# 108 tiny zero products among TensorE's first filler in an RWKV attention and spatial-gating kernel

## The chip, the cores and the metric

The kernel runs on one core of one Trainium2 chip. The time is device microseconds from one launch to the end. Besides the timed runs there is one profiled execution; the trace, from which all rows below are taken, is of that execution.

## The reference

Two stages follow each other. The first is a linear recurrence with a decay per channel, over 4 batches, 8 heads, 768 steps and 48 channels a head:

```
cur   = (u * k_t) outer v_t
y_t   = r_t . (state + cur)
state = w_t * state + k_t outer v_t
```

The second takes y as x (768 rows of 384 values per batch) and is a gated two-layer network with mixing along the sequence:

```
h = relu(x @ w_in);  u, v = halves of h
v_n = (v - mean(v)) / sqrt(var(v) + 1e-6)
v_s = w_spatial @ v_n + b_spatial          (along the 768 steps)
out = (u * v_s) @ w_out
```

## The kernel before

The recurrence is cut into chunks of 128 steps, so there are 24 slots (4 batches of 6 chunks). A slot turns the decays into running products with two scans on VectorE (L442, L452), scales k and r by them (L455, L457), transposes k on TensorE (L514, tile pt), forms the state's increments (L572, tile pp), the scores within a half chunk (L497, tile pp), and adds state and score products into the tile pyw (L526). The slots up to the sixth also do a small product for the bonus term (L427, tile pg). For the first eight slots TensorE helps to form the low part of the result (L621). After each slot its rows go through the second half of w_in (tile ph, L631 to L633: each product of full precision is made of three, from high and low parts). When a batch's six chunks are there, the first half of w_in (tile pu), the spatial mixing (tile pv), the gate and w_out (tile po) follow. The weights are split into high and low parts on the chip as they arrive (tiles d_, e_, wi, ws, wo).

Nothing is decided at run time. The long table PLAN gives each of the program's operations an engine and a start time, `plan` sorts them, and `issue` writes them in that order to five instruction streams; SyncE's stream issues all loads and stores, in order, each after the operation that frees its buffer.

One thing is put between: `fill`. It walks through the sorted operations and, where the plan leaves TensorE idle, calls `warm(n)` for n products of zeros: a load of the zero tile zk and a bf16 product of 128 x 320 into pw, a part of the pyw tile that nobody reads. 73 such products stand in the program, all in its first sixth; the first 23 stand at the very start, before the first transposes of slot 0. They are instructions as any other: TensorE does them in order, whether or not it would have been idle.

TensorE's stream is by far the longest: 6019 weight loads and 6019 matmuls in the trace. An fp32 product of the program is two loads and two matmuls there (the 16 products of L572 in a slot are 32 matmuls), a transpose, an fp32r or a bf16 product is one of each.

Of the kernel before, what the change touches and what calls it, by code (L numbers as in the profile page):

```python
# [116 lines left out]
GAP, FILL_TO = 0.2, 5  # L117

WINDOW, DUTY, UNIT = 3.41, 0.95, 0.15

EARLY = 8

# [8 lines left out]
Q = 32  # L131
# [84 lines left out]
def kernel(  # L216
# [14 lines left out]
    nc = tc.nc  # L231
# [39 lines left out]
    pw = pyw[:, :, KX:, :].rearrange("p x a t -> p x (a t)")  # L271
# [597 lines left out]
    count = [0]  # L869

    def warm(n):
        z = zk.bitcast(BF16)
        for _ in range(n):
            nc.tensor.matmul(pw[:, count[0] % 2], z[:, :P], z[:, :pw.shape[-1]], start=count[0] < 2, stop=True,
                             skip_group_check=True)
            count[0] += 1

    def fill(order):
        t, runs = 1.9, []

        def busy(a, b):
            return sum(max(0.0, min(e, b) - max(s, a)) for s, e in runs)

        for o in order:
            if o.on == "T":
                s, took = o.start, o.eng["T"]
                if t < last.start:
                    n = int(min((DUTY * WINDOW - busy(s - WINDOW, s)) / UNIT + 0.99, (s - t - GAP) / UNIT))
                    if n > 0:
                        warm(n)  # L890
                        runs.append((t, t + n * UNIT))
                runs.append((s, s + 0.85 * took))
                t = max(t, s + took)
            yield o

    def range_check():
# [17 lines left out]
        return bad  # L914

    op({"T": 0.1}, lambda: warm(1), w=[("pw", 0)])
    for j in range(2):
        op({"S": 0.45}, lambda j=j: nc.sync.dma_start(
# [6 lines left out]
    for i in range(NS):  # L925
# [22 lines left out]
        if i == FILL_TO:  # L948
            prog.last = last = op({"T": 0.1}, lambda: warm(1), r=[(vn[0, c][0], 0)], w=[("pw", 0)])
# [72 lines left out]
```

## Time and profile before

| | us |
|---|---|
| median of 3 runs (lowest to highest) | 372.14 (371.58 to 374.35) |
| the profiled execution's own time | 373.94 |
| its span, first to last instruction | 372.2 |
| TensorE matmuls busy | 356.9 (96%), x6019 |
| VectorE busy | 246.9 (66%) |
| ScalarE busy | 192.0 (52%) |
| GpSimd busy | 112.6 (30%) |
| DMA, read and written over the span | 126 GB/s |

The profiled execution is 1.80 us slower than the median of the runs, and 1.7 us lie outside its span. Busy times of TensorE overlap from one instruction to the next, so a busy share of 96% does not say that it could not be faster; idle time ahead of an instruction, and what ended it, is read from the timeline.

### The profile page before, as it was taken

How to read it: one execution, taken by the hardware profiler on the slowest of the kernel's cores; microseconds unless marked ns; L12 is line 12 of the kernel's file. 1: busy time of each engine (PE TensorE's matmuls, PEld its weight loads, DVE VectorE, ACT ScalarE, POOL GpSimd, SP SyncE). 2: the span in 40 equal slices, each digit the busy share in tenths (PEclk: the TensorE clock that was granted, in tenths of full speed). 3: DMA queues.
4: the chain of work that ended last, by engine and by line, in shares of the span. 5: the costliest groups of instructions: out<-in, count | busy, mean ns of one | idle time of the engine just before them, and what ended most of it. 6: DMA issues, size and time to landing. Idle time of an engine off the chain costs nothing.

```text
span 372.2 us, 13843 instructions
## 1 busy us (share of the span) xinstructions
PE 356.9 (96%) x6019; PEld 320.0 (86%) x6019; DVE 246.9 (66%) x486; ACT 192.0 (52%) x517; POOL 112.6 (30%) x141
## 2 busy tenths in 40 slices
PE   7699899999999999999999989999999999999995
PEld 4467678899889998998989978999899998999995
DVE  7869969998895875947837767748648571323231
ACT  2648788996347378731644348551445074622122
POOL 2427431023235043273064330380351034021030
PEclk9969999999999999999999999999999999999999
DMA  8857756684543545342534545325423150110211
GB/s 198 258 149 212 221 174 214 195 239 125 163 132 98 179 143 173 111 140 70 160 94 123 169 137 162 95 78 153 140 66 94 44 155 4 37 49 0 91 39 67
DMA packets 33024, 47.91 MB, mean 129 GB/s; under 512 B 3265, under 2 KB 21825, under 8 KB 32961
## 3 DMA queue, kind: packets, MB, share of 16 engines
q1 hardware_dynamic: 32960, 47.00, 43.2%
q8 instruction: 48, 0.79, 0.9%
q14 instruction: 16, 0.12, 0.1%
HBM read 42.27 MB, written 4.72 MB: 126 GB/s over the span
## 4 chain that ended last, share of the span: by engine, by line
PE 81%; DMA 8%; issue 3%; DVE 2%; ACT 2%; SPq 1%; POOL 1%; POOLq 0%; DVEq 0%; ACTq 0%
PE pv L631 9%; PE pyw L526 9%; PE pv L632 8%; PE pv L633 8%; PE po L631 5%; PE po L633 5%; PE po L632 5%; PE ph L631 4%; PE pu L631 4%; PE ph L633 4%; PE ph L632 4%; DMA rr<-in_tr_dram 4%; PE pu L632 4%; PE pu L633 4%; PE pp L497 4%
## 5 line engine op out<-in xcount | busy, mean ns | idle before, releaser
L631 PE MATMUL pv<-ws,vh 128*128 128x384 f32 x192 | 67.0, 349 | 0.4 <-DVE t L737 0.3
L632 PE MATMUL pv<-ws,vh 128*128 128x384 f32 x192 | 64.9, 338 | 0.0
L633 PE MATMUL pv<-ws,vl 128*128 128x384 f32 x192 | 64.8, 338 | 0.0
L737 DVE TENSOR_TENSOR t<-pv,b_sb 128x384 f32<-128x384 f32 x32 | 17.5, 552 | 36.7 <-PE pv L633 34.5
L631 PEld LDWEIGHTS pv<-ws,vh 128*128 128x128 f32 x192 | 36.0, 188 | 2.0 <-DVE t L737 0.5
L632 PEld LDWEIGHTS pv<-ws,vh 128*128 128x128 f32 x192 | 36.1, 188 | 0.2
L633 PEld LDWEIGHTS pv<-ws,vl 128*128 128x128 f32 x192 | 36.0, 188 | 0.0
L631 PE MATMUL pu<-xT,wi 128*128 128x384 f32 x96 | 33.9, 353 | 0.2 <-DVE dg L469 0.2
L631 PE MATMUL po<-wo,gh 128*128 128x384 f32 x96 | 33.1, 345 | 0.0
L632 PE MATMUL pu<-xT,wi 128*128 128x384 f32 x96 | 32.5, 338 | 0.0
L633 PE MATMUL pu<-xT,wi 128*128 128x384 f32 x96 | 32.4, 338 | 0.0
L633 PE MATMUL po<-wo,gl 128*128 128x384 f32 x96 | 32.3, 337 | 0.0
L632 PE MATMUL po<-wo,gh 128*128 128x384 f32 x96 | 32.3, 337 | 0.0
L500 DVE COPY_PREDICATED As<-mask,pp 128x512 f32<-128x512 int32 x24 | 17.7, 739 | 19.2 <-POOL As L483 6.0
L442 DVE TENSOR_TENSOR_SCAN F<-W,zz 112x512 f32<-112x512 f32 x24 | 29.1, 1212 | 1.9 <-ACT zz L454 1.0
L631 PE MATMUL ph<-wi,xT 128*128 128x512 f32 x72 | 30.0, 417 | 0.0
L452 DVE TENSOR_TENSOR_SCAN W<-W,zz 112x512 f32<-112x512 f32 x24 | 29.1, 1213 | 0.4
L741 ACT CAST gh<-t 128x384 fp32r<-128x384 f32 x32 | 16.1, 510 | 25.5 <-POOL t L739 16.1
L633 PE MATMUL ph<-wi,xT 128*128 128x512 f32 x72 | 28.4, 395 | 0.0
L632 PE MATMUL ph<-wi,xT 128*128 128x512 f32 x72 | 28.3, 394 | 0.0
L599 POOL TENSOR_TENSOR SA<-S,prod 112x256 f32<-112x256 f32 x18 | 13.9, 773 | 44.8 <-DVE S L597 39.9
L660 ACT ACTIVATE hv<-ph 128x512 f32<-128x512 f32 x24 | 14.3, 597 | 25.4 <-PE ph L633 25.4
(184 smaller groups left out, 824.6 us busy)
## 6 DMA issues: line engine op xcount, KB each, us to landing
N<-in_nat_dram SPq DMA_DIRECT2D x18, 384.0 KB, 3.5
Nw<-in_gt_dram SPq DMA_DIRECT2D x16, 384.0 KB, 3.6
W<-in_tr_dram SPq DMA_DIRECT2D x24, 224.0 KB, 3.9
kk<-in_tr_dram SPq DMA_DIRECT2D x24, 224.0 KB, 3.2
rr<-in_tr_dram SPq DMA_DIRECT2D x24, 224.0 KB, 3.6
v<-in_nat_dram SPq DMA_DIRECT2D x24, 192.0 KB, 3.5
out_dram<-ot SPq DMA_DIRECT2D x24, 192.0 KB, 3.3
wst<-in_w_spT_dram SPq DMA_DIRECT2D x12, 192.0 KB, 3.8
```

The source lines that it names most:

```text
L442: op({"V": 1.22}, lambda: nc.vector.tensor_tensor_scan(flat(F())[:, ::-1], W[:, 2:][:, ::-1], flat(zz[:R])[:, ::-1], 0.0, ALU.mult, ALU.ma ...
L452: op({"V": 1.22}, lambda: nc.vector.tensor_tensor_scan(W[:, :n], W[:, :n], flat(zz[:R]), 0.0, ALU.mult, ALU.max), r=[("zz", 0)], w=[wk])
L497: nc.tensor.matmul(pa[ts, j, g, :], kk()[rs, g, ts], rr()[rs, g, ts], start=True, stop=True)
L500: op({"V": 0.73}, lambda: nc.vector.copy_predicated(As().rearrange("p (g j) t -> p j g t", j=2), mask.unsqueeze(1).unsqueeze(1).broadcast_ ...
L526: nc.tensor.matmul(py[Q * n:Q * (n + 1), x, k_, :], a, b, start=(x, n) not in seen, stop=True, skip_group_check=True)
L599: op({"V": 0.42, "G": 0.617}, lambda e: e.tensor_tensor(new, S0, Wc.unsqueeze(2).broadcast_to([R, G, E2]), ALU.mult), r=[("S0",), ("Wc", i ...
L631: nc.tensor.matmul(ps, ah, bh, start=first, stop=False)
L632: nc.tensor.matmul(ps, ah, bl, start=False, stop=False)
L633: nc.tensor.matmul(ps, al, bh, start=False, stop=last)
L660: op({"A": 0.69}, lambda: nc.scalar.activation(hv(), ph(), AF.Relu, accum_out=col(0)), r=[(ph, 0)], w=[(hv, 0), (s, 0, j)])
L737: op({"V": dve(HT)}, lambda: nc.vector.tensor_tensor(t1(), pv()[:, :HT], b_sb[:, tsl], ALU.add), r=[(pv, 0), ("b", 0)], w=[(t1, 0)])
L741: op({"A": act(HT)}, lambda: nc.scalar.copy(gh(), t1()), r=[(t1, 0)], w=[(gh, 0)])
```

## The change

After the 13th zero product, and after each one up to the 21st, the function `ahead` writes 12 tiny products: 32 rows, 32 columns and 32 moving elements of the same zero tile, in bf16, going round the four diagonal 32 x 32 squares of the array, into the same unread part of pyw. That makes 9 x 12 = 108 more loads and 108 more matmuls, 216 instructions, in TensorE's stream, all within the first 21 of its 23 opening zero products. No other stream and no data change.

```diff
+AHEAD_FROM, AHEAD = 13, 9
...
     def warm(n):
         z = zk.bitcast(BF16)
         for _ in range(n):
             nc.tensor.matmul(pw[:, count[0] % 2], z[:, :P], z[:, :pw.shape[-1]], start=count[0] < 2, stop=True,
                              skip_group_check=True)
             count[0] += 1
+            if AHEAD_FROM <= count[0] < AHEAD_FROM + AHEAD:
+                ahead(z)
+
+    def ahead(z):
+        for k in range(12):
+            k = k % 4 * Q
+            nc.tensor.matmul(pw[k:k + Q, count[0] % 2, :Q], z[k:k + Q, :Q], z[k:k + Q, :Q], start=False, stop=True,
+                             skip_group_check=True)
```

TensorE's stream where the opening zero products end and slot 0 begins, before (L874 is the zero product, pt the transposes, pg the bonus product):

```order
L874 LDWEIGHTS zk
L874 MATMUL pyw<-zk 128x320
L514 MATMUL pt_195<-ident,kk_147 128x112 x4
L427 MATMUL pg_200<-up_sb,rk_169 128x2 x4
```

The same place now, from the last of the tiny products (L884; all lines below are 1 or more further down):

```order
L884 LDWEIGHTS zk
L884 MATMUL pyw<-zk 32x32
L875 LDWEIGHTS zk
L875 MATMUL pyw<-zk 128x320
L875 LDWEIGHTS zk
L875 MATMUL pyw<-zk 128x320
L515 MATMUL pt_303<-ident,kk_147 128x112 x4
L428 MATMUL pg_308<-up_sb,rk_169 128x2 x4
```

The last tiny one stands ahead of the last two zero products; the transposes follow as before.

TensorE's stream where slot 0 ends (L526) and slot 1's increments of the state (L572) are made, before:

```order
L526 MATMUL pyw<-As_236,vp_122 32x64 x16
L526 MATMUL pyw<-As_236,v_152 32x64 x16
L526 MATMUL pyw<-rr_150,SA_127 32x64 x8
L572 MATMUL pp<-v_163,KT_341 48x48 x16
L427 MATMUL pg_374<-up_sb,rk_234 128x2 x4
L621 MATMUL pyw<-xT_0_0_371,nident 128x192 x2
```

And now:

```order
L527 MATMUL pyw<-As_344,vp_122 32x64 x16
L527 MATMUL pyw<-As_344,v_152 32x64 x16
L527 MATMUL pyw<-rr_150,SA_127 32x64 x8
L573 MATMUL pp<-v_163,KT_449 48x48 x16
L428 MATMUL pg_482<-up_sb,rk_342 128x2 x4
L622 MATMUL pyw<-xT_0_0_479,nident 128x192 x2
```

Nothing has changed places here; everything has 108 more matmuls ahead of it (324 in place of 216 before L572 begins, counted as the trace counts them).

## Rows read from the trace of the kernel before

**Rows 1.** The page: span, and TensorE's granted clock in 40 slices.
```profile
span 372.2 us, 13843 instructions
...
PEclk9969999999999999999999999999999999999999
```

**Rows 2.** The waits: engine, line, what ended the wait; us, times, longest.
```profile
PE pp L572 <- issue: 2.7, 1, 2.7
```

**Rows 3.** The DMA queues, whole span: packets, MB, share of 16 engines.
```profile
q8 instruction: 48, 0.79, 0.9%
```

**Rows 4.** Stretches 0:18.1 and 18.1:47.1: busy (count) by engine, clock, DMA, GB/s.
```profile
0.00:18.10 18.10, 12.86 (x221) 8.54 (x221) 14.50 (x28) 8.15 (x21) 6.31 (x23) 1.00 0.84 226
18.10:47.10 29.00, 25.88 (x635) 19.68 (x635) 24.69 (x44) 19.67 (x59) 13.37 (x10) 0.88 0.66 193
```

**Rows 5.** The DMA queues from 0 to 15.4 (no q8 row there).
```profile
q1 hardware_dynamic: 3090, 3.67, 88.7%
```

**Rows 6.** Queue q8 in tenths of a us from 15.4, 22.4, 44.4 and 48.9.
```profile
q8 instruction: 1, 0.02, 77.8%
...
q8 instruction: 1, 0.02, 67.1%
...
q8 instruction: 1, 0.02, 84.1%
...
q8 instruction: 1, 0.02, 58.2%
```

**Rows 7.** TensorE's timeline: start, us, instruction xcount, idle before it and its releaser.
```profile
1.16 5.55 PE L874 MATMUL pyw<-zk 128*128 128x320 bf16 x23 [1.16 <-DVE zk L261]
7.69 0.57 PE L514 MATMUL pt<-ident,kk 112*128 112x112 f32 x4 [0.98 <-DVE kk L455]
...
9.93 1.40 PE L874 MATMUL pyw<-zk 128*128 128x320 bf16 x9
...
11.61 0.69 PE L497 MATMUL pp<-rr,kk 48*64 48x64 f32 x32
...
13.01 0.60 PE L514 MATMUL pt<-ident,kk 112*128 112x112 f32 x4 [0.46 <-POOL kk L455]
...
15.17 0.29 PE L572 MATMUL pp<-v,KT 64*48 64x48 f32 x5
18.13 0.56 PE L572 MATMUL pp<-v,KT 64*48 64x48 f32 x27 [2.67 <-issue]
...
21.04 3.62 PE L874 MATMUL pyw<-zk 128*128 128x320 bf16 x13 [0.69 <-ACT xT L624]
24.59 0.68 PE L526 MATMUL pyw<-rr,SA 48*32 48x64 f32 x32
25.20 1.13 PE L497 MATMUL pp<-rr,kk 48*64 48x64 f32 x32
```

**Rows 8.** SyncE's timeline: the loads issued around the first instruction packet.
```profile
6.05 0.35 SPq L337 DMA_DIRECT2D d_('wv', 2)_165<-in_w_in_dram  x1
...
10.35 0.43 SPq L337 DMA_DIRECT2D d_('wv', 1)_247<-in_w_in_dram  x1
12.37 0.33 SPq L394 DMA_DIRECT2D kk<-in_tr_dram  x1
```

**Rows 9.** DMA issues by tile: KB, median us from issue to landing.
```profile
d_('wv', 1)_247<-in_w_in_dram SPq DMA_DIRECT2D x1, 512.0 KB, 6.7
```

**Rows 10.** VectorE's timeline: the small copy that waits for pg.
```profile
9.32 0.16 DVE L469 COPY dg<-pg 128x8 f32<-128x8 f32 x1
```

**Rows 11.** The stretch 19.4:26.3, columns as in rows 4.
```profile
19.40:26.30 6.90, 6.21 (x83) 4.00 (x83) 3.72 (x8) 4.51 (x14) 1.66 (x1) 0.51 0.49 163
```

**Rows 12.** TensorE's timeline from 45 us, and SyncE's from 41 us.
```profile
47.17 0.45 PE L526 MATMUL pyw<-rr,SA 48*32 48x64 f32 x29 [1.84 <-issue]
...
41.67 0.42 SPq L922 DMA_DIRECT2D b_sb<-in_b_rep_dram  x1
42.99 0.33 SPq L394 DMA_DIRECT2D kk<-in_tr_dram  x1
```

## The prediction

> **What bounds the kernel now.** I read the page first. TensorE shows work in nearly every slice of the span, and its granted clock is full in every slice but one near the start, the third, at 6 tenths [rows 1]. So the end of the kernel is a long chain of matmuls whose order is fixed, and a change to the first 20 us can be worth only what it takes from, or adds to, TensorE's idle or slow time there. The second view is the list of waits: the longest one of TensorE that no semaphore ended is 2.7 us, in front of L572 [rows 2]. The timeline puts it at 15.46 to 18.13: five of the 32 matmuls of slot 1's L572 run, then nothing, then the other 27 [rows 7].
>
> The DMA queues tell what this wait is. Queue q8 carries instructions alone: 48 packets, 0.79 MB, so 16.5 KB each [rows 3]. TensorE has 12038 loads and matmuls (front table, twice 6019); over 48 packets that is 251 each, or about 127 pairs with the few semaphore instructions counted in. No q8 packet runs in the first 15.4 us; the first starts at 15.4, just as TensorE stops [rows 5, 6]. TensorE goes on 2.7 us later. The same happens again: the packet that starts at 44.4 is followed by TensorE's start at 47.17 after 1.84 us of nothing [rows 6, 12], again 2.7 us later. Between the two stops lie 635 matmuls, which is 5 x 127 [rows 4]. So both are the end of a block of about 127 load and matmul pairs with the next one not yet there. At the first, 221 pairs were done [rows 4].
>
> When is a block asked for? After the stop, block three is entered at 18.13; the next packet starts at 22.4 [rows 6], with the 27 of L572 and more behind it. After the stop that ended at 47.17 the next one starts at 48.9 [rows 6]. That fits one request on entering a block, for the block after it, which then takes its turn behind loads already given to the queues: 4.3 us and 1.7 us there. The first request would have been made on entering the block that ended after pair 221, so after pair 94, at the end of the nine zero products at 9.93 to 11.3 [rows 7]. SyncE had by then issued a load of 512 KB at 10.35 that took 6.7 us to land [rows 8, 9], and 3.67 MB had moved when the packet started [rows 5]. So a wait of 4 to 5 us for that turn.
>
> **The change, part by part.** The sum is made against the profiled execution, 373.94 us, which is 1.80 above the median of 372.14.
>
> The 108 tiny products. Nearest rows: 32 matmuls of L526, also on small squares, in 0.68 us at the lower clock, 21 ns each; 32 of L497 in 1.13 us there and 0.69 us at full clock, 35 and 22 ns [rows 7]. They have 64 columns and fp32; the tiny ones 32 and bf16, so I take 12 to 21 ns: 1.3 to 2.3 us, 1.8 taken. The 23 zero products take 5.55 us, 0.24 each, between the 0.28 of the half clock (13 in 3.62) and the 0.16 of the full one (9 in 1.40) [rows 7]: the clock rises under way, and about three more of them would come after its rise: 0.3 off. The transposes at 7.69 waited 0.98 us [rows 7], so TensorE is late by 1.8 - 0.3 - 1.0 = 0.5 us (0 to 1.1). Behind it pg is late, and VectorE's copy of it at 9.32 [rows 10], and what follows there to slot 0's last matmuls. So L572 of slot 1 starts at 15.7 in place of 15.17. Whatever it is, the next wait absorbs it.
>
> The block ends. 13 zero products, and then groups of 12 tiny and one: pair 94 is now in the seventh group. 13 at 0.27 and six groups at 0.4 from 1.16 give 7 us, so the first request leaves some 3 to 4 us sooner. The load issued at 6.05 [rows 8] is the last ahead of it, and the packet should start between 8.5 and 11 and TensorE have its block 2.7 us later, at 11 to 13.7. The end after pair 221 now lies at old pair 113, 18 matmuls into slot 0's L497, which ran from 11.61 [rows 7]. So there a wait of 0 to 1.5 us; behind it stand the transposes that waited for GpSimd until 13.01 anyway [rows 7]. I take nothing on the path.
>
> The next end is after pair 348, old pair 240. Slot 1's L572 begins after old pair 216 (the second place in the order), so this end stands after the 24th of its 32 matmuls, where it stood after the 5th. **The first block comes sooner, but another now ends 19 matmuls behind the old stop.** Its request leaves on entering the block at old pair 113, at 11.5 to 13.5 us. The 512 KB load of 10.35 is before it either way, slot 2's kk of 12.37 [rows 8] perhaps. By the old packet's start its turn comes at 15.4 to 16.5, and TensorE can go on at 18.1 to 19.2. I take 18.2: as before, with 8 matmuls left where 27 took 0.56 us [rows 7]. L572 ends at 18.4, not 18.69: **-0.2 us**, between -2.1 (no wait at all) and +0.7.
>
> The clock. After the old stop the granted clock reads 0.51 from 19.4 to 26.3 [rows 11], the 1.2 GHz level for nearly all of it. There 13 zero products took 3.62 us (2.0 at 0.16 each), and L497 took 1.13 where it takes 0.69 [rows 7]: 1.6 + 0.4 = 2.0 us, on the path, since slot 1's scores come only behind them. 373.94 - 2.0 = 371.9 is near the fastest run of 371.58, which fits runs in which the clock did not fall. The new stop runs from 16.1 (24 matmuls from 15.7) to 18.2, so 2.1 us. The stop of 1.84 us left the clock up, since the only slices below 9 tenths end before 28 us [rows 1, 12]; that of 2.67 did not. 2.1 is nearer to 1.84, so I take **-2.0 us**, with 0 as the other end.
>
> Later ends. All stand 19 to 20 pairs further on in the work, after one packet more. At 45.33 the stop had 29 matmuls of L526 behind it [rows 12]; the new one comes 0.3 us later among the same, and its request about 0.5 us later, among small matmuls too: **+0.2 us**, between -1.8 (it is gone) and +2.7 (rival 3). Where the matmuls are large, a block lasts longer than a fetch, and a shift costs nothing.
>
> Sum: 373.94 - 0.2 - 2.0 + 0.2 = 371.9; **371.9 us**, 0.2 under the median.
>
> A rule that speaks against it: the Trainium skill, page "Runtime: NRT & Kernel Launch", section "Instruction fetch mechanics", says that blocks of 16 KiB hold 256 instructions, that the next is fetched while the current one runs, and that crossing a boundary is mostly hidden. The block size agrees with the 251 above. The hiding does not hold where small matmuls pass in 16 ns (29 in 0.45 us [rows 12]): the trace shows 2.67 and 1.84 us. By the rule no wait would be there to move, and the sum would be rival 4's.
>
> **Rivals.**
> 1. The clock falls all the same, since 2.1 us is still a long stop: 371.9 + 2.0 = 373.9. Chance 0.20.
> 2. The wait goes. The packet for the block after old pair 240 gets its turn within 2 us, as at 48.9, because the queue takes instruction packets between loads. L572 then ends at 16.6: 373.94 - 2.1 - 2.0 + 0.2 = 370.0; if the stop at 45.33 goes too, 368.0. For it: 1.7 us at 48.9. Against: 4.3 us at 22.4 and the long turn of the first. Chance 0.17, of which 0.06 for the lower time.
> 3. Slower: the stop at 45.33 grows. Its request, made some 0.5 us later, falls behind b_sb's load (41.67) and kk's (42.99) [rows 12], 128 x 768 and 112 x 512 values in fp32, so 0.62 MB, or 2.7 us at 226 GB/s [rows 4]. The stop is then 4.5 us, over the 2.67 that brought the clock down once, and that costs 2.0 more: 371.7 + 2.7 + 2.0 = 376.4. It decides from a stop of about 2.5 us. Chance 0.11.
> 4. The change does not do what it says: the stop is tied to L572, not to a count of instructions, and stays after the 5th matmul at 2.67 us, 0.5 us later: 374.4. Against: 5 x 127. Chance 0.05.
>
> **The numbers.** The forecast has 0.47, at 371.9, own range 370.6 to 373.2. To leave out no more than 2 in 10, the range takes rivals 1 and 4 and the upper time of rival 2, and half of rival 3: 368.6 to 375.2. A difference under 1% (3.7 us) is about what a measurement of this kernel can't tell from none. Faster by over 1% (under 368.4): the lower time of rival 2 and the forecast's own tail, 0.12. Slower by over 1% (over 375.9): half of rival 3 and some of 1 and 4 with a longer filler, 0.09. Same: 0.79.
>
> **What would show it.** A q8 packet between 8 and 11.5 us and a second at 15 to 17; TensorE idle, without a releaser, between the 24th and 25th matmul of slot 1's L572, until about 18.2; the tiny ones at 12 to 21 ns; the clock full from 19 to 26. It is wrong if the second packet starts before 14 us, if the first filler ends after 9.5, or if the stop near 45 is over 2.5 us long.

## The result and the profile after

| | us |
|---|---|
| the change, median of 20 runs (lowest to highest) | 377.09 (373.80 to 382.47) |
| the kernel before, median of 20 runs beside it | 373.78 (371.53 to 381.51) |
| ratio, 95% interval | 1.0070 (1.0041 to 1.0099) |
| the profiled execution of the change, its span | 381.21, 379.5 |

So the change is slower by some 0.7%, where 371.9 and no change were forecast, and 377.09 lies above the range. The sum of the forecast started from the profiled execution's 373.94, which is 0.16 above the median of 20 runs of the kernel before, 373.78. So nearly all of the 5.19 us between forecast and median are the change's: 2.04 that the sum took off and the medians do not show, and 3.31 that came on top. The ratio leaves out executions more than 1.5% above their kernel's fastest, the medians do not. The profiled execution of the change took 4.1 us more than its median, so what the change does is read below from two further profiles of it as well.

The page of the change, as [rows 1, 3]:

```profile
span 379.5 us, 14059 instructions
...
PEclk9989975999999999999999999999999999999999
...
q8 instruction: 49, 0.80, 0.9%
```

One instruction packet more. The lowest slices of the clock are now the sixth and seventh, 47 to 66 us; before it was the third, which is now at 8 tenths. TensorE's timeline, as [rows 7, 12]:

```profile
1.16 3.65 PE L875 MATMUL pyw<-zk 128*128 128x320 bf16 x13 [1.16 <-DVE zk L262]
4.74 0.27 PE L884 MATMUL pyw<-zk 32*32 32x32 bf16 x12
...
5.32 0.26 PE L884 MATMUL pyw<-zk 32*32 32x32 bf16 x12
...
10.03 0.95 PE L515 MATMUL pt<-ident,kk 112*128 112x112 f32 x4
...
14.09 2.58 PE L875 MATMUL pyw<-zk 128*128 128x320 bf16 x9
...
17.18 0.69 PE L498 MATMUL pp<-rr,kk 48*64 48x64 f32 x32
...
20.08 0.57 PE L573 MATMUL pp<-v,KT 64*48 64x48 f32 x32
...
48.97 0.32 PE L527 MATMUL pyw<-rr,SA 48*32 48x64 f32 x9 [1.83 <-issue]
...
198.71 0.32 PE L527 MATMUL pyw<-rr,SA 48*32 48x64 f32 x9 [0.26 <-issue]
...
233.53 0.26 PE L527 MATMUL pyw<-As,vp 64*32 64x64 f32 x5 [0.31 <-issue]
```

Nine zero products take 2.58 us at 14.09 where they took 1.40: in this execution TensorE's products take the times of the lower of its two clocks through all of its opening, up to 17 us. (This is read from the products. The clock column reads 1.00 from 9.5 to 17.1 us here, and in the opening of the kernel before as well, where 23 zero products took 0.24 us each [rows 4, 7]; so it does not show the opening's level.) The transposes come at 10.03 in place of 7.69, slot 0's L498 at 17.18 in place of 11.61. There is no stop left in slot 1's L573, because everything is so late that the block is there. Three stops without a releaser remain: near 49, and two that the kernel before did not have, at 198 and 233 us. The first instruction packet, in the tenth of a us from 10.2, and two stretches at the lower clock (columns as [rows 4]):

```profile
q8 instruction: 1, 0.02, 68.8%
```

```profile
24.00:27.30 3.30, 3.30 (x48) 1.77 (x49) 2.22 (x4) 2.58 (x9) 1.60 (x1) 0.50 0.99 330
...
51.30:64.80 13.50, 13.50 (x175) 11.08 (x178) 9.42 (x21) 8.49 (x23) 3.96 (x5) 0.50 0.57 163
```

The second stretch at 0.50 follows the stop of 1.83 us and lasts 13.5 us; the fall of [rows 11] is shorter here, 3.3 us in place of 6.9.

### The profile page after: what moved, and what is told of

Read it like the earlier page. It is cut to its first block, busy times and chain, and to the rows that moved or that the text cites. A ratio compares the mean times of both kernels' runs of the same rounds, so it can differ in the third digit from the quotient of the medians.

```text
span 379.5 us, 14059 instructions
## 1 busy us (share of the span) xinstructions
PE 367.2 (97%) x6127; PEld 327.2 (86%) x6127; DVE 247.4 (65%) x486; ACT 193.0 (51%) x517; POOL 114.2 (30%) x141
## 4 chain that ended last, share of the span: by engine, by line
PE 84%; DMA 5%; DVE 5%; ACT 2%; issue 2%; POOL 1%; ACTq 0%; POOLq 0%; DVEq 0%; SPq 0%
PE pv L632 8%; PE pyw L527 8%; PE pv L633 8%; PE pv L634 8%; PE po L632 5%; PE ph L632 5%; PE po L634 4%; PE po L633 4%; PE pu L632 4%; PE ph L634 4%; PE ph L633 4%; PE pu L633 4%; PE pu L634 4%; PE pp L498 4%; PE pyw L875 3%; PE pt L515 2%
## 5 line engine op out<-in xcount | busy, mean ns | idle before, releaser
L632 PE MATMUL pu<-xT,wi 128*128 128x384 f32 x96 | 34.5, 359 | 0.0
L633 PE MATMUL pu<-xT,wi 128*128 128x384 f32 x96 | 33.0, 344 | 0.0
L634 PE MATMUL pu<-xT,wi 128*128 128x384 f32 x96 | 33.0, 343 | 0.0
L632 PE MATMUL ph<-wi,xT 128*128 128x512 f32 x72 | 30.8, 428 | 0.0
L634 PE MATMUL ph<-wi,xT 128*128 128x512 f32 x72 | 29.1, 405 | 0.0
L633 PE MATMUL ph<-wi,xT 128*128 128x512 f32 x72 | 29.1, 404 | 0.0
L527 PE MATMUL pyw<-rr,SA 48*32 48x64 f32 x1408 | 25.7, 229 | 2.2 <-issue 2.1
```

What stands on the lines that cost most here:

```text
L527: nc.tensor.matmul(py[Q * n:Q * (n + 1), x, k_, :], a, b, start=(x, n) not in seen, stop=True, skip_group_check=True)
L632: nc.tensor.matmul(ps, ah, bh, start=first, stop=False)
L633: nc.tensor.matmul(ps, ah, bl, start=False, stop=False)
L634: nc.tensor.matmul(ps, al, bh, start=False, stop=last)
```

## The experiments

Four theories are meant by letters from e8 on. A: small products spread among the large zero products keep the clock low in the opening, and that is the price (A2: the spreading has a price beside the ends). C (in e8's expectation B): the places of the later block ends decide. D: the ends in slots 0 and 1 decide. E: each tiny product costs. Names or letters in the expectations of e1 to e7 are those expectations' own. "Old pair n" is TensorE's n-th matmul of the kernel before; ratios are to runs of the kernel before that were taken beside those of the variant. A stop is idle time of TensorE that no semaphore ended (`issue`). The lines shown are picked from each timeline; not all that lies between them is marked. All of them:

| kernel | tiny products | ends as with | median | ratio (95% interval) |
|---|---|---|---|---|
| the change | 108 spread | 108 | 377.09 | 1.0070 (1.0041 to 1.0099) |
| e7, the same | 108 spread | 108 | 378.68 | 1.0082 (1.0038 to 1.0126) |
| e14, the same | 108 spread | 108 | 376.81 | 1.0055 (1.0012 to 1.0098) |
| e1 | 108 spread, 128 x 128 | 108 | 374.86 | 1.0000 (0.9962 to 1.0039) |
| e2 | 108 behind the 23rd | 108 | 375.20 | 1.0000 (0.9965 to 1.0036) |
| e15, as e2 | 108 behind the 23rd | 108 | 376.45 | 1.0058 (1.0022 to 1.0094) |
| e10 | 86, and 22 behind slot 0's L498 | 108 | 378.04 | 1.0063 (1.0009 to 1.0118) |
| e12 | 86, and 22 behind slot 1's L622 | 108 from 19 us | 375.59 | 1.0021 (0.9974 to 1.0068) |
| e3 | 86 behind the 23rd | 86 | 373.72 | 0.9941 (0.9900 to 0.9983) |
| e9, as e3 | 86 behind the 23rd | 86 | 371.57 | 0.9939 (0.9908 to 0.9970) |
| e8 | 86 spread | 86 | 372.54 | 0.9945 (0.9908 to 0.9981) |
| e11 | 128 behind the 23rd | before | 372.28 | 0.9926 (0.9888 to 0.9964) |
| e13 | 108 spread, 20 behind the 23rd | before | 372.28 | 0.9992 (0.9947 to 1.0036) |
| e4 | 10 in place of 10 zero products | before | 372.43 | 0.9962 (0.9920 to 1.0004) |
| e5 | e3, and 50 pairs more later | other | 375.65 | 0.9961 (0.9914 to 1.0009) |
| e6 | none, two loads later | before | 374.70 | 0.9994 (0.9952 to 1.0037) |

**e1, whole-array tiny products.**

```diff
-            k = k % 4 * Q
-            nc.tensor.matmul(pw[k:k + Q, count[0] % 2, :Q], z[k:k + Q, :Q], z[k:k + Q, :Q], start=False, stop=True,
+            nc.tensor.matmul(pw[:, count[0] % 2, :Q], z[:, :P], z[:, :Q], start=False, stop=True,
```

> The change with its 108 tiny products made 128 x 128 x 32 in place of 32 x 32 x 32: same number, same places, same instruction blocks, 32 moving columns as before, but the whole array at work. Theory H (the tiny products held the granted clock at half from 5.8 to 17.1 us, and that, not their own time alone, made slot 0 late): if more of the array at work lets the clock rise, it is full by about 9.5 us, the opening filler ends near 9 us in place of 9.8, slot 0's L498 ends at 14 to 15 us in place of 17.9, and the time falls by 2 to 3 us against the change. If the clock counts only how long columns stream, it stays at half and the kernel is as slow as the change. Rival H2 (the 216 instructions themselves are the loss, the clock is incidental): L498 ends at 17 to 18 whatever the clock reads. Rival H3 (the loss comes later, from block ends near 47 us and the clock's fall behind them): the start may gain and the total stays within 0.5 us of the change.

Measured: 1.0000. The ends lie as in the change and the transposes were late by 1.6 us. It is 0.7% under the change's ratio, but the intervals nearly touch, so by itself it decides little. Slot 0's L498 was done at 13.9 us, sooner than H had it; but e7 and e14, the change itself, are done with it at 14.2 and 13.9, so this does not show an effect of the whole array either. Its stop near 45 was 1.67 us, and the clock fell behind it as in the change.

**e2, all 108 behind the 23rd zero product.**

```diff
-            if AHEAD_FROM <= count[0] < AHEAD_FROM + AHEAD:
-                ahead(z)
+            if count[0] == 23:
+                for m in range(108):
+                    ahead(z, m)
```

> The same 108 tiny products, but all behind the 23rd zero product, when the clock of the kernel before had risen (5.8 us) and TensorE was idle for 0.98 us. Every later block end lies where the change has it. H: the clock is full from 5.8 us on; 108 products at 12 to 15 ns end at 7.8 to 8.3 us; the transposes start then (before 7.69, change 10.03), slot 0's L498 ends at 12.5 to 13.2 us, and slot 1's L573 meets the stop that the prediction put after its 24th matmul, until 17.5 to 18.5 us, if it meets one at all; total 0 to 3 us under the kernel before, 4 to 6 under the change. H2: transposes at 9.5 or later, total as the change. H3: the start gains but the stop at 47 us and a fall of the clock behind it remain, total within 1 us of the change.

Measured: 1.0000 here; the same text gave 1.0058 as e15. Four of TensorE's stops, in its timeline:

```profile
13.30 0.46 PE L498 MATMUL pp<-rr,kk 48*64 48x64 f32 x14 [1.53 <-issue]
17.42 0.30 PE L573 MATMUL pp<-v,KT 64*48 64x48 f32 x7 [0.96 <-issue]
...
192.39 0.32 PE L527 MATMUL pyw<-rr,SA 48*32 48x64 f32 x9 [0.64 <-issue]
226.66 0.26 PE L527 MATMUL pyw<-As,vp 64*32 64x64 f32 x5 [0.84 <-issue]
```

The first two stops stand where the prediction put them, with 14 of L498 left, as forecast, and 7 of L573, not 8. The last two are new. With a time like that of the kernel before, the run does not decide between its expectation's three theories.

**e3, 86 behind the 23rd.** As e2 with `range(86)`.

> 86 tiny products behind the 23rd zero product. Counting by 127 pairs, block ends then lie at old pair 135 (among the four zero products before slot 0's L526) and 262 (among the 13 zero products behind L622), both where TensorE works through large zero products. H, with the reading of the block ends: no stop in slot 1's L573, it ends at 16 to 16.8 us (before 18.69), no fall of the clock before 40 us, total 2 to 4 us under the kernel before. H2: no better than the kernel before, since 172 instructions cost 2 us. H3: the total depends on the later block ends, which lie 22 pairs from those of the change; any sign, without regard to slot 1.

Measured: 0.9941, faster than both kernels; e9 repeats it with 0.9939. What e9's timeline shows is told there.

**e4, ten zero products made tiny**, no block end moved.

```diff
-            nc.tensor.matmul(pw[:, count[0] % 2], z[:, :P], z[:, :pw.shape[-1]], start=count[0] < 2, stop=True,
-                             skip_group_check=True)
+            if 13 <= count[0] < 23:
+                ahead(z, count[0])
+            else:
+                nc.tensor.matmul(pw[:, count[0] % 2], z[:, :P], z[:, :pw.shape[-1]], start=count[0] < 2, stop=True,
+                                 skip_group_check=True)
```

> The clock alone: the kernel before, with zero products 14 to 23 made tiny (32 x 32 x 32). The number of instructions and all block ends are as before; TensorE is free sooner, at about 5 us, and waits for k at 7.69. H: the granted clock is not up at 5.8 us, and stays at half until the next zero products at 10 to 17 us have run; pt, pg, L573 and nine zero products take twice their time, slot 0's L498 ends 1.5 to 4 us later than 12.30; the stop after the 5th matmul of slot 1's L573 stays and ends at 18 to 19 us, so that most of it is absorbed and the total is 0 to 1.5 us over the kernel before. H2: no added time, so everything as before or sooner. H3: as before within 0.5 us.

Measured: 0.9962. In its profile L498 of slot 0 came 3 us late, at the lower clock, and yet:

```profile
14.60 0.69 PE L498 MATMUL pp<-rr,kk 48*64 48x64 f32 x32
...
17.50 0.57 PE L573 MATMUL pp<-v,KT 64*48 64x48 f32 x32
```

L573 ran whole and was done at 18.07, before's 18.69 [rows 7]. A start 3 us late costs nothing there, since TensorE stood 2.67 us for the block anyway. So the prediction's "whatever it is, the next wait absorbs it" holds up to about that size. The 0 to 1.5 us over the kernel before that theory H expected did not come in the median of its runs; the profiled execution, with falls of the clock later on, was the longest of the 12 (377.99).

**e5, a second shift later on.** e3, and in its 13 zero products behind slot 1's L622 the last four replaced by 54 tiny ones:

```diff
+            if 49 <= count[0] < 53:
+                for m in range(13 + count[0] % 2):
+                    ahead(z, m)
+            else:
```

> The tail of 86 tiny products, and in the filler of 13 zero products behind slot 1's L622 the last four made 54 tiny ones: 50 pairs more, in about the time of the four. Block ends behind lie 136 pairs, that is one block and 8 pairs, from those of the kernel before. By times between block ends (each end's request to the next end, against a fetch of up to 6 us) the stops of the tail of 86 at 35.5 (1.53 us) and 46 us (1.12 us) go or shrink under 0.5 us, and none comes that is longer than 1 us. If the falls of the clock near 47 us come from such stops, they come more rarely: total 1 to 3 us under the tail of 86, 3 to 5 under the kernel before. If they come from something else, the total is within 1 us of the tail of 86. If 54 tiny products in a row bring the clock down themselves, 2 to 3 us over it.

Measured: 0.9961, no faster than e3 and e9, so the 1 to 3 us under them did not come. The two stops of e3 that it was to cure are gone from their places, but two others over 1 us came, 1.40 at 45.58 and this one right behind the added products:

```profile
25.49 0.83 PE L428 MATMUL pg<-up_sb,rk 112*128 112x2 f32 x7 [3.12 <-issue]
```

**e6, the packet's turn.** The kernel before with the 512 KB loads d_wu0 and d_wv1 issued later, behind slot 2's kk: two words of PLAN.

```diff
-... V20q Sub V1fq ...
+... V20q S12m V1fq ...
-... A1fi St2 V1am ...
+... A1fi S11i V1am ...
```

> The kernel before, but two loads of 512 KB (tiles d_wu0 and d_wv1, issued at 9.81 and 10.35) moved behind the load of slot 2's kk, so that they are issued at about 12.8 us. Theory Q (the instruction packet takes its turn behind loads already issued): the first packet starts at 11 to 12.8 us in place of 15.45, the block is there at 14 to 15.5, and the stop in slot 1's L572 is gone or under 0.3 us; the next packet starts before 20 us. L572 ends at 15.7 to 16.2. The weights come 2 to 3 us later, which the split of d_wu0 on VectorE feels (it ran at 16.65); total 0 to 3 us under the kernel before. Rival (the packet is asked for only when the block has run out): packet at 15.4 and stop of 2.5 us as before, total the same or 1 us more.

Measured: 0.9994. With the loads away the first packet started at 11.9, not 15.45, and the stop in L572 was gone, but:

```profile
14.64 0.57 PE L572 MATMUL pp<-v,KT 64*48 64x48 f32 x32
...
21.17 3.62 PE L874 MATMUL pyw<-zk 128*128 128x320 bf16 x13 [4.67 <-ACT xT L624]
```

L572 was done at 15.2, 3.5 us sooner than in [rows 7], and the zero products behind it, which waited 0.69 us for ScalarE before, now wait 4.67 and start where they did (21.04). ScalarE's timeline tells why:

```profile
18.65 0.77 ACT L353 ACTIVATE d_('wu', 0)_294<-d_('wu', 0)_294,third 128x512 int32<-128x512 uint8 x1 [3.42 <-DMA d_('wu', 0)_294<-in_w_in_dram]
...
20.65 0.46 ACT L624 CAST xT<-pyw 128x384 fp32r<-128x384 f32 x1
```

The load that made way for the packet is now waited for itself, and xT stands behind it on ScalarE. The run shows that a packet's turn comes behind loads already issued, and nothing on what the stop is worth. For that e9 serves (below): no stop in L573, no load moved, and the 13 zero products start at 18.55, 2.5 us sooner than before.

**e7, the change once more.**

> The change itself once more, for a second trace and more times. H (clock held at half until 17 us): the granted clock again is at half until 14 to 18 us, slot 0's L498 ends at 16 to 18.5 us, slot 1's L573 has no stop and ends 1.5 to 2.5 us later than in the kernel before (18.69), and where the clock does not fall after 45 us the span is 2 to 3 us over the kernel before. H3 (later block ends are the loss): in such an execution the distance to the kernel before at L573 is under 1 us and grows behind 45 us. Ratio 1.004 to 1.010 by both.

Measured: 1.0082, so the loss is real. This time the clock rose in the opening at about 5.9 us. Its stops:

```profile
13.71 0.46 PE L498 MATMUL pp<-rr,kk 48*64 48x64 f32 x14 [0.41 <-issue]
17.55 0.30 PE L573 MATMUL pp<-v,KT 64*48 64x48 f32 x7 [0.69 <-issue]
45.31 0.32 PE L527 MATMUL pyw<-rr,SA 48*32 48x64 f32 x9 [1.66 <-issue]
...
194.63 0.32 PE L527 MATMUL pyw<-rr,SA 48*32 48x64 f32 x9 [0.38 <-issue]
211.77 0.42 PE L527 MATMUL pyw<-rr,SA 48*32 48x64 f32 x22 [0.62 <-issue]
230.01 0.26 PE L527 MATMUL pyw<-As,vp 64*32 64x64 f32 x5 [1.52 <-issue]
```

```profile
46.90:60.50 13.60, 13.60 (x137) 11.62 (x136) 9.66 (x21) 8.61 (x24) 4.11 (x5) 0.50 0.57 165
231.20:234.60 3.40, 3.40 (x9) 2.63 (x9) 3.03 (x6) 1.72 (x7) 0.00 (x0) 0.50 0.48 125
```

Old pair 856 is reached at 43.22, before it was 45.12: the opening has won 1.9 us. Then the clock is at 0.50 for 13.6 us, and the last of the stops is followed by another fall. The slow opening of the first profile is thus not needed for the loss.

**e8, 86 spread as in the change.**

```diff
-        for k in range(12):
+        for k in range(10 if count[0] < 18 else 9):
```

> The change with 86 tiny products in place of 108, spread as in the change (9 or 10 after each zero product from the 13th to the 21st); from the opening's end on, its stream is that of the version with 86 of them behind the 23rd zero product. Theory A (the loss of the change comes from the spreading: small products between the large zero products delay the rise of TensorE's clock in some executions, and slot 0 then runs at the half clock): slower than the 86 behind the filler by 0.6 to 1.0%, so a ratio to the kernel before of about 1.000 to 1.005; where the profiled execution opens slowly, the transposes start after 9 us and slot 0's L498 ends after 14. Theory B (only the number counts, because it sets where the blocks end): a ratio of 0.990 to 0.998, as the 86 behind the filler had.

Measured: 0.9945, as the 86 behind the filler. Its profiled execution opened as slowly as that of the change (transposes at 9.97, L498 done at 17.8), and yet the ratio is outside theory A's range. That one execution was the longest of the 12, 378.19. How many executions open slowly is not known, so what a slow opening costs in the execution that has it is left open; the ratio shows that the spreading of 86 has no such price as A forecast.

**e9, e3 again on e8's chip.**

> The 86 tiny products behind the 23rd zero product, once more, on the same chip as the spread 86. By either theory 0.990 to 0.998 of the kernel before, if the 0.994 was no accident of one chip; no stop in slot 1's L573, the transposes at 7 to 8 us, L498 of slot 0 ended by 12.5, and stops after old pairs 643 and 897.

Measured: 0.9939. Its stops:

```profile
25.72 0.37 PE L527 MATMUL pyw<-As,v 64*32 64x64 f32 x19 [0.52 <-issue]
36.81 0.21 PE L527 MATMUL pyw<-As,v 64*32 64x64 f32 x1 [1.29 <-issue]
46.86 0.61 PE L428 MATMUL pg<-up_sb,rk 112*128 112x2 f32 x5 [1.12 <-issue]
...
63.90 0.35 PE L527 MATMUL pyw<-As,v 64*32 64x64 f32 x17 [0.89 <-issue]
...
223.90 0.35 PE L527 MATMUL pyw<-As,v 64*32 64x64 f32 x18 [0.44 <-issue]
```

The sixth, left out here, is 0.31 us at 58.02. There are as many as in e7, none of them in L573, and one of 0.44 us where e7 has three between 190 and 235 us. Slot 1's L573, and the zero products behind its L622:

```profile
15.14 0.57 PE L573 MATMUL pp<-v,KT 64*48 64x48 f32 x32
...
18.55 2.88 PE L875 MATMUL pyw<-zk 128*128 128x320 bf16 x13 [1.55 <-ACT xT L625]
```

**e10, 86 and 22 later.** e3, and one later zero product replaced by 22 tiny ones (`if count[0] == 35`).

> The version with 86 tiny products behind the 23rd zero product, and 22 more in place of the first of the 13 zero products behind slot 1's L622. Up to there it is the version with 86 (0.994 of the kernel before); from there on all block ends lie where the change with 108 has them (old pairs 876, 1128, 3546, 4183). Theory C (the place of the later block ends decides): it loses what the 86 won, a ratio of 0.999 to 1.008, with a stop of 1.4 to 1.9 us after old pair 876. Theory D (the opening decides: with 108 ends lie inside slot 0's L498 and near the end of slot 1's L573, with 86 neither): it stays at 0.990 to 0.997 with L573 of slot 1 ended by 15.6 us and no stop in it.

Measured: 1.0063. I had miscounted the fillers: the 22 stood behind slot 0's L498, so one block also ended inside slot 1's L573, with a stop of 2.36 us (18.39). The stop after old pair 876 was 1.06 us, under the 1.4 to 1.9 of C. The ratio therefore fits C, but does not speak against D.

**e11, a whole block of 128.** As e2 with `range(128)`.

> 128 tiny products behind the 23rd zero product: a whole block of them, so that all later block ends lie again where the kernel before has them (old pairs 221, 856, 1109), but each one packet later. Theory C (the later ends decide): like the kernel before, a ratio of 0.997 to 1.004, with a stop after old pair 856 as there. Theory E (each tiny product costs, whatever lies where, so that 108 lose and 86 do not): slower than the change, 1.009 or more. Theory D: the opening now has an end after the 5th matmul of L573 again, with a request that leaves sooner than before's; a stop there of 0.5 to 2 us, and a ratio of 0.996 to 1.002.

Measured: 0.9926. Theory E is out: more tiny products than in the change, and faster than the kernel before by 0.7%. C and D missed too: their lowest ratios, 0.997 and 0.996, lie above the measured one. The stop in L573 lies after the 5th matmul again, as [rows 7] had it, and is 1.26 us long:

```profile
17.36 0.56 PE L573 MATMUL pp<-v,KT 64*48 64x48 f32 x27 [1.26 <-issue]
```

**e12, the 22 where e10 meant them** (`if count[0] == 40`).

> As the run before with 22 later, but these 22 tiny products now do stand in place of the first of the 13 zero products behind slot 1's L622; the run before had them behind slot 0's L498, so that a block still ended near the end of slot 1's L573. Theory C (the later ends decide): from there on the ends lie as in the change, the stops after old pairs 3546 or 3801 and 4183 (near 193, 211 and 227 us) come back, 0.4 to 1.5 us each, and the ratio to the kernel before is 0.998 to 1.008. Theory D (the ends in slots 0 and 1 decide, which are as with 86 here): 0.990 to 0.997.

Measured: 1.0021, inside C's range and above D's: the opening of the fast version with the later ends of the change has lost 0.8% against e3 and e9, on another chip. All ends from 19 us on are moved here, so it does not tell the one near 45 from those near 190 and 225. Of its stops, the first here has its like in e9, the last two are those of the change:

```profile
37.03 0.54 PE L527 MATMUL pyw<-As,v 64*32 64x64 f32 x19 [2.01 <-issue]
...
190.84 0.32 PE L527 MATMUL pyw<-rr,SA 48*32 48x64 f32 x8 [0.49 <-issue]
224.85 0.26 PE L527 MATMUL pyw<-As,vp 64*32 64x64 f32 x4 [0.39 <-issue]
```

**e13, the change and 20 more.**

```diff
+            if count[0] == 23:
+                ahead(z, 20)
```

> The change as it is, its 108 tiny products spread as they are, and 20 more behind the 23rd zero product: 128, a whole block, so that the later ends lie again where the kernel before has them. Theory C (the later ends decide): 20 more products make the change faster, 0.990 to 1.000 of the kernel before, and no stop near 194, 211 and 227 us. Theory A (small products spread among the large zero products keep TensorE's clock low in the opening, and that is the price): as the change, 1.004 to 1.012. Theory E (each tiny product costs): 1.008 or more.

Measured: 0.9992, theory C's range and neither A's nor E's. In the whole stretch up to 250 us two stops without a releaser are left (a third, 1.09 us, comes at 299.19):

```profile
45.96 0.45 PE L527 MATMUL pyw<-rr,SA 48*32 48x64 f32 x29 [1.56 <-issue]
58.35 0.35 PE L527 MATMUL pyw<-rr,SA 48*32 48x64 f32 x16 [0.39 <-issue]
```

Slot 1's L573 runs whole, and the clock falls behind it all the same: it reads 0.50 from 19.2 to 25.8 us.

```profile
16.73 0.80 PE L573 MATMUL pp<-v,KT 64*48 64x48 f32 x32
...
20.08 3.63 PE L875 MATMUL pyw<-zk 128*128 128x320 bf16 x13 [1.26 <-ACT xT L625]
```

**e14 and e15, the change and e2 side by side on one chip.**

> The change itself, on the same chip as the version with its 108 tiny products behind the filler, for a direct comparison. All block ends of the two lie alike. Theory C (the ends alone decide): both alike, 1.001 to 1.007, with mean granted clocks that do not differ. Theory A2 (the spreading has a price of its own, since more executions then run with a low clock): the change at 1.004 to 1.012, with half or more of its executions under a mean granted clock of 0.984 (19 of 32 so far; a quarter of those of the kernel before).

> 108 tiny products behind the 23rd zero product, on the same chip as the change. Theory C: as the change, 1.001 to 1.007. Theory A2: 0.996 to 1.004, 0.5% or more under the change, with a third of its executions or fewer under a clock of 0.984 (4 of 12 so far).

Measured: 1.0055 and 1.0058, with 5 of 12 executions under a mean clock of 0.984 in each. That is against A2: side by side, where the 108 stand makes no difference that can be seen, and the 0.6% between e2 and e15, which are the same text, shows how far such comparisons scatter. (With 128 the spread ones of e13 are 0.7% over those of e11, on different chips and with intervals that overlap, so a small price is not ruled out there.) e14's profiled execution, 372.80 us, is one of the shortest of the change, 4.0 under its median; its span is 371.1 us, 1.1 less than that of the kernel before [rows 1]:

```profile
8.35 0.55 PE L515 MATMUL pt<-ident,kk 112*128 112x112 f32 x4
...
12.25 0.56 PE L498 MATMUL pp<-rr,kk 48*64 48x64 f32 x18
13.46 0.46 PE L498 MATMUL pp<-rr,kk 48*64 48x64 f32 x14 [0.65 <-issue]
...
16.11 0.51 PE L573 MATMUL pp<-v,KT 64*48 64x48 f32 x25
17.58 0.30 PE L573 MATMUL pp<-v,KT 64*48 64x48 f32 x7 [0.96 <-issue]
...
20.14 1.93 PE L875 MATMUL pyw<-zk 128*128 128x320 bf16 x13 [0.97 <-ACT xT L625]
...
44.30 0.32 PE L527 MATMUL pyw<-rr,SA 48*32 48x64 f32 x9 [1.99 <-issue]
```

```profile
4.40:45.20 40.80, 35.44 (x985) 26.84 (x984) 37.57 (x64) 26.76 (x79) 17.77 (x14) 1.00 0.80 224
45.30:52.00 6.70, 6.70 (x54) 5.72 (x53) 4.40 (x10) 5.88 (x16) 1.55 (x3) 0.50 0.62 183
```

Here the forecast's opening can be seen almost as it was written, and what became of it: the clock does not fall at 19 us, the 13 zero products take 1.93 us in place of 3.62, old pair 856 comes at 41.88, 3.2 us sooner. Then the stop of 1.99 us, a fall of the clock from 45.3 to 52, and old pair 1109 comes at 57.70, only 1.0 sooner than before (58.74).

**What the later ends cost.** From the start times of the same matmuls in every profile: between old pairs 3540 and 3560, 3780 and 3810, 4180 and 4190 (near 194, 212 and 229 us, rows of small L527 matmuls) the kernel before takes 1.1, 0.3 and 0.1 us. The change takes 1.6, 0.3 and 0.6 in its first profile, 1.7, 1.2 and 1.8 in e7, 1.6, 0.7 and 0.6 in e14. In all eight profiles with the ends of 108 the three together are 1.1 to 3.2 us longer than in the kernel before; in the eight others (e3 to e6, e8, e9, e11, e13) by no more than 0.25, but for e6 with 0.85. These have a stop elsewhere: 0.5 to 0.9 us more than before between old pairs 4190 and 4300 with 86, 0.6 and 0.8 more than before between 4780 and 4800 with 128. Part of the loss at the three places is made up between them: the whole stretch from old pair 3500 to 4310 takes 42.8 us before, 43.9, 46.1 and 42.9 in the three profiles of the change, 43.5 in the middle of the eight with ends of 108, and 42.2 in the middle of the eight others. So of the 1.8 us in the middle at the three places some 0.7 (against the profile before) to 1.3 (against the others) are left behind them.

**The clock.** A fall behind the stop near 45 us costs 4 to 5 us: old pairs 900 to 1109 take 9.3 us before, 14.1 and 13.7 in the two profiles of the change in which it lasted 13.5. Executions with a mean granted clock under 0.984: 24 of 44 of the change, 37 of 145 of the kernel before, 16 of 42 in the other kernels with all 108 ends (e1, e2, e10, e15), 9 of 36 with 86, 2 of 18 with 128 (e11, e13), but also 6 of 12 in e4, which moves no end, and 2 of 12 in e12. Among the 44 they are 4.4 to 4.7 us longer than the others, by the medians of each of the three sets of runs. In executions at 0.984 or more, the change is 1.1 us (e7) and 2.2 us (e14) over the kernel before beside it, by the medians: so there is a loss without a long fall of the clock too.

## Why the prediction was wrong

**Where the block ends lie, and who asks for what.** Right. The first packet started at 10.2 (8.5 to 11 forecast), the stop in L498 comes after its 18th matmul, that in L573 near its end, with 7 left and not 8. (Old pair 94 is not the end of the nine zero products but the 15th of the 16 matmuls of L526 behind them, at 11.3 to 11.6 us; that changes nothing in the rest.) In e14 TensorE goes on at 17.58 (18.2 forecast) and is done with L573 at 17.88 (18.4). The stop near 45 stands 20 pairs further on, 1.99 us long in e14 and 1.83 in the first profile, against the 1.84 + 0.2 of the sum.

**The tiny products.** At the full clock a group of 12 and one zero product takes 0.42 us in e14, so (0.42 - 0.16) / 12 = 22 ns each, just above 12 to 21. That is the price of standing among the large ones: 86 of them in a row took 0.83 us in e9, 10 ns each. The transposes come 0.66 late in e14 (0.5, up to 1.1). In the first profile the clock stays low, a group takes 0.57 us, and they come 2.3 late. The text's own sign, "the first filler ends after 9.5", came out so; but e7, where the transposes come 1.2 late and the loss is as large, and e8's ratio show that the loss does not need it.

**L573, -0.2 us, and the clock behind it, -2.0 us.** Both happened in e14 and neither lasted. 3.2 us were won up to old pair 856, and 2.2 of them lost again by old pair 1109. In e7, e2 and e15 the clock fell at 18 to 20 us all the same, behind stops in L573 of only 0.7 to 1.3 us, and in e9 and e13, which have no stop there, it reads 0.50 from 19.5 to 22.7 and from 19.2 to 25.8: the comparison of 2.1 with 1.84 and 2.67 decided nothing, and the -2.0 did not hang on that stop. That was rival 1, 373.9, about what the kernel before takes. That the old stop was on the path is shown by e9, where it is gone and 2.5 us are won behind it; the change won less at that place, since its second stop leaves the 13 zero products at 20.1 us.

**The step that failed**, beside this -2.0, and the one that put the time above the range, is the one on the later ends: "Where the matmuls are large, a block lasts longer than a fetch, and a shift costs nothing." The premise was read from the first 60 us and carried to the other 310, and there too every slot has its small matmuls. The kernel before passes the three places near 194, 212 and 229 us in 1.5 us; with the 108 products, blocks end there, and it takes 1.1 to 3.2 us more. That moving the ends costs time is shown by e12, which lost 0.8% against e3 and e9 with the same fast opening, and the other way by e13, which took the loss back with 20 products more. Both move the end near 45 together with the others, so how the loss is shared between them is argued from the profiles. The term was +0.2, and only for the end near 45. It should have been a sum over all the ends, some 48.

**Rival 3** had the right place and the wrong condition. The stop near 45 does not have to grow to bring the clock down: with 1.83, 1.66, 1.99, 1.64 and 1.67 us (change, e7, e14, e15, e1) it fell, with 1.44, 1.06 and 1.03 (e2, e10, e12) it did not, but the kernel before stood 1.84 and e6 1.92 without a fall, and e4 1.90 and e3 1.12 with one: the length of the stop does not decide it. A mean clock under 0.984 stands for a long fall in the count above (e14's fall of 6.7 us is too short for it), and the change's executions have it twice as often, 55% and 26%; at 4.5 us each that is 1.3 us of the 3.3 between the medians. With the 0.7 to 1.3 us that the later ends leave, some 2 to 2.6 us are accounted for, and the rest is open. The share is counted, the cause of it not shown: no run moved the stop near 45 alone, and e4 has the long falls as often with its ends as before.

**The rule that was weighed.** The Trainium skill, page "Runtime: NRT & Kernel Launch", section "Instruction fetch mechanics", has it that crossings of a block's boundary are mostly hidden. By number that agrees with the runs, 3 to 6 visible stops for 49 packets in the profiles of the change. By time it misleads here: the six of e7 add up to 5.3 us, 1.4% of its span, more than the whole effect of the change. The three of the kernel before add up to 4.9 us, so the sum of the visible stops alone does not tell the loss.

**Chances.** 0.09 stood on slower by over 1%, 0.79 on within 1%. By the ratio, 0.7%, it is the latter; against the 372.14 by which the 1% was set the median is 1.3% up, and the range ended 1.9 us short of it.

## What to carry to other kernels

An edit that only adds instructions to a stream moves every later block end of that engine, so list all of them against the stretches of small instructions over the whole program, not only the one that is to be cured. The number to add is then a free parameter: here 86 won 0.6%, 108 lost 0 to 0.8%, and 128 won 0.7% in one run and nothing clear of its interval in the other, while where they stood among the fillers made no difference that could be measured side by side (e8 and e9, e14 and e15). And a stop that is cured is worth what is left of it at the end of the program: the 3.2 us that one execution had won by 42 us were 1.0 us at 58.

## What was not expected of the hardware

The clock's opening differs from one execution to the next of the same program: in the three profiles of the change TensorE's products went over to the times of the higher clock at about 17, 6 and 4 us, and 12 tiny products with one zero product took 0.57 us before that and 0.42 after it. An execution that is spared an early fall may have one at the next stop, as in e14, so that what a cured stop wins at once is not what the kernel wins.
